# A written table of task order for a linear-attention and MLP kernel, with its streamed tiles at one address phase

## The chip, the cores and the metric

The kernel runs on one core of a Trainium2 chip. The metric is the device time of one execution in microseconds (us). Engines are named as in the profile: PE multiplies matrices (PEld loads its weights), DVE, ACT and POOL work element by element, SP issues most DMAs.

## The reference

```python
def _attn_ref(r, k, v, w, u):             # B, H, S, D = 4, 8, 768, 48
    for t in range(S):
        cur = einsum('bhd,bhe->bhde', u * kt, vt)
        y[:, :, t] = einsum('bhd,bhde->bhe', rt, state + cur)
        state = wt[..., None] * state + einsum('bhd,bhe->bhde', kt, vt)

def _moe_ref(x, w_in, w_out):             # x: 3072 x 384, d_ff = 2048
    h = x @ w_in
    g = where(h > 0, h, exp(min(h, 0)) - 1)
    return g @ w_out

# reference: x = attention output as (B*S, H*D), then _moe_ref
```

## The kernel before

The sequence is cut into 6 chunks of 128 steps. With 4 batch entries that makes 24 **units** (`units`, number i = 4 x chunk + batch). The tokens of one chunk are one MLP **step** of N = 512 columns; the hidden layer is cut into NF = 16 slices f of 128. In chunks 0 and 1 the first six slices are done in two halves of 256 columns (`FH`), so that the MLP can begin when two of the four units are there. That makes 108 pairs of MLP blocks, numbered n = 0 to 107: n = 0 to 21 are chunk 0, 22 to 43 chunk 1, and then 16 for each chunk.

A unit is a set of tasks on several engines. `es` and `gs` (DVE scans, L359 and L369) make decays from the loaded `w`; `rkc` (DVE, L395) makes products for the diagonal in units 0 to 7, `rk` and `rku` (POOL) in the others; `kh` and `rh` (DVE, L376, L373) scale k and r; `pd` (PE, L400), `md` and `sp` (ACT, or POOL) make the diagonal matrix `am`; `s` (PE, L430) makes the scores in `pa_s`; `mk` (DVE, L433, two halves) masks them into `am`; `t` (PE, L438) transposes k and `kt` (ACT, L442) copies it out; `v` (PE, L460) makes the output `pa_y` from `am`, v and the state `st`; `xh` and `xl` (ACT, DVE L470) split it into the two parts that the MLP streams; `u` (PE, L477), `sc` and `up` (DVE) update the state.

An MLP pair is `g1` (PE, L234: nine matmuls into `ph`), `r1` and `r2` (ACT), `stt` (DVE, L245), which together are the ELU, `gh` (ACT, L249) and `gl` (DVE, L253), the split of its result, and `g2` (PE, L264: nine matmuls into `acc`). A product of two fp32 numbers is made of three: high x high, high x low, low x high. The weights are converted once: `raw` loads two tiles of slice f, `a` (ACT, L510), `cc` (DVE, L514, tile `wg`), `wh` (ACT, L518) and `wl` (DVE, L521) make `w_h` and `w_l`, which stay.

What sets the order: every task is entered in `Plan` with its engine, an assumed duration (`COST`), what it follows (`after`) and the buffer slots it takes (`hold`; `SLOTS` says how many there are: 2 of `ph`, `m`, `gh`, `gl`, `w`, 3 of `k`, `r` and of the PSUM tag `pa`, on which `pd`, `s`, `t`, `v`, `u` all draw). `Plan.order` runs a list scheduler over them: each engine takes the ready task with the earliest latest start, worked out from the due times `BEGINS` of the chunks. The kernel is emitted in that order. On the chip an engine runs its own tasks strictly in that order and waits on semaphores; nothing is reordered at run time.

`warm` (L336) is ten matmuls of the identity at the start. For the last chunk `out` copies three tiles of `acc` and issues the stores itself (L269 to L278): tile 0 copied by ACT and issued by SP, tile 1 by DVE and SP, tile 2 in two halves, the first by ACT and ACT's queue, the second by DVE and SP. `guard` and `flags` watch for decays out of range; `general` is a slow path that is not taken here.

Of the kernel before, what the change touches and what calls it, by code (L numbers as in the profile page):

```python
# [54 lines left out]
COST = dict(es=1.5, gs=1.4, pc=0.2, pd=0.6, md=0.22, spa=2.4, rh=0.62, kh=0.62, rk=0.48, rku=0.48, prk=1.1, prku=1.1, dg=0.5, mk=0.7, up=0.7, sc=0.5, xl=0.48,  # L55
            cand=0.5, cv=0.9, wl=0.9, stt=0.6, gl=0.64, fl=1.4, kt=0.5, xh=0.46, a=0.87, wh=0.8, r1=0.58, r2=0.6, gh=0.6,
            sp=1.7, s=1.15, t=0.5, v=1.75, v0=1.1, u=0.5, g=2.12, out=0.6)
LAT = 0.06
DMA_FIRST, DMA_ISSUE, DMA_LAT, DMA_RATE = 1.0, 0.45, 1.9, 215.0
BEGINS = (14.0, 109.9, 197.8, 304.8, 356.4, 464.7, 493.9)  # L60
SOON = 0.0
HALF = 0.0
STAY = 0.0
SWITCH = 0.0
MODES = dict(s=1, v=2, u=3, pd=4)
# [7 lines left out]

class Plan:


    def __init__(self):
        self.tasks, self.holds, self.queue = {}, {}, {}

    def add(self, key, eng, dur, fn, after=(), due=None, start=0.0, lock=False, size=0):  # L80
        self.tasks[key] = dict(key=key, eng=eng, dur=dur, fn=fn, after=list(after), due=due, start=start, lock=lock, size=size)

    def hold(self, pool, taker, users, n=1, fifo=True):
        if taker not in self.tasks:
# [4 lines left out]

    def order(self):  # L90
        ts = self.tasks
        succ = {k: [] for k in ts}
        for k, t in ts.items():
            t["after"] = [d for d in t["after"] if d in ts]
            for d in t["after"]:
                succ[d].append(k)
# [682 lines left out]
```

## Time and profile before

| | us |
|---|---|
| median of 3 runs | 546.36 (544.46 to 551.71) |
| the profiled execution | 549.48 |
| its span, first to last instruction | 547.8 |
| PE busy in it | 521.6 (95%) |
| DVE busy | 338.9 (62%) |
| ACT busy | 287.0 (52%) |
| POOL busy | 66.9 (12%) |

Granted clock of PE over the span: 0.986. DMAs moved 47.34 MB, 86 GB/s on average, but 245 to 297 GB/s in the first 27 us. A busy share is an average over stages with different limits, and matmuls that overlap in the pipeline keep PE "busy" also where it runs at half its rate; so the stages have to be read one by one. In the rows below, "x9" behind a PE row is one MLP block, and a bracket at a row's end is the idle time of the engine before it and what ended it.

### The profile page before, as it was taken

What the parts mean: (1) busy time and instruction counts of PE and PEld (TensorE: products, weight loads), DVE (VectorE), ACT (ScalarE), POOL (GpSimd) and SP (SyncE); (2) the same over time, 40 slices, a digit from 0 to 9 for tenths busy, and PEclk for the clock granted to TensorE, in tenths of its full rate; (3) what the DMA queues carried; (4) which work ended last, traced back from release to release, by engine and by line L of the source; (5) the groups of instructions that cost most, each with busy time, mean ns of one, the idle gap of its engine ahead of it and who ended that gap; (6) DMA issues with size and microseconds to landing.
All of it is one profiled execution on the core that took longest, in us unless ns stands there. A gap on an engine that the chain in (4) does not pass through costs nothing.

```text
span 547.8 us, 9962 instructions
## 1 busy us (share of the span) xinstructions
PE 521.6 (95%) x4065; PEld 431.6 (79%) x4065; DVE 338.9 (62%) x533; ACT 287.0 (52%) x558; POOL 66.9 (12%) x74
## 2 busy tenths in 40 slices
PE   6987999999999998899999999998999999999994
PEld 6776998889888886778888788886778887888883
DVE  5779899966695357994528833357983339333331
ACT  3777899747465434454543634434454453444442
POOL 2000000000620013612005100007300000000000
PEclk9997999999999999899999999999999999999998
DMA  8966661114510026730003400034410012010001
GB/s 245 297 199 212 201 224 67 34 53 151 165 37 2 0 78 184 231 92 17 17 1 109 134 16 1 0 113 150 157 53 1 1 23 70 12 46 1 0 1 62
DMA packets 26739, 47.34 MB, mean 86 GB/s; under 512 B 2752, under 2 KB 9280, under 8 KB 26688
## 3 DMA queue, kind: packets, MB, share of 16 engines
q1 hardware_dynamic: 26544, 46.52, 27.7%
q8 instruction: 34, 0.56, 0.4%
q14 instruction: 17, 0.14, 0.1%
q10 hardware_dynamic: 144, 0.13, 0.1%
HBM read 41.92 MB, written 4.72 MB: 85 GB/s over the span
## 4 chain that ended last, share of the span: by engine, by line
PE 81%; DMA 8%; DVE 6%; issue 2%; ACT 1%; SPq 1%; POOL 0%; DVEq 0%; ACTq 0%
PE ph L234 35%; PE acc L264 34%; PE pa_y L460 6%; DMA k<-in_wkr_dram 5%; PE pa_s L430 3%; DMA wrawx<-in_w_out_dram 1%; DMA wrawx<-in_w_in_dram 1%; PE pa_t L438 1%; PE pa_u L477 1%; DVE eg L359 1%; PE pa_d L400 1%; DVE m L245 1%; DVE k L376 1%; DVE am L433 1%; DMA wraw<-in_w_out_dram 1%
## 5 line engine op out<-in xcount | busy, mean ns | idle before, releaser
L245 DVE SCALAR_TENSOR_TENSOR m<-m,ph 128x512 f32<-128x512 f32 (+1 forms) x108 | 67.1, 624 | 117.5 <-ACT m L242 117.2
L239 ACT ACTIVATE m<-ph 128x512 f32<-128x512 f32 (+1 forms) x108 | 59.3, 549 | 128.8 <-PE ph L234 121.0
L234 PE MATMUL ph<-xh,w_h 128*128 128x512 f32 (+1 forms) x324 | 122.5, 378 | 2.7 <-DVE m L245 2.3
L264 PE MATMUL acc<-gh,w_h 128*128 128x512 f32 (+1 forms) x325 | 122.0, 375 | 0.0
L234 PE MATMUL ph<-xh,w_l 128*128 128x512 f32 (+1 forms) x324 | 120.7, 372 | 1.0 <-DVE w_l L521 1.0
L234 PE MATMUL ph<-xl,w_h 128*128 128x512 f32 (+1 forms) x324 | 120.6, 372 | 0.0
L264 PE MATMUL acc<-gl,w_h 128*128 128x512 f32 (+1 forms) x325 | 120.0, 369 | 0.0
L264 PE MATMUL acc<-gh,w_l 128*128 128x512 f32 (+1 forms) x325 | 119.7, 368 | 0.0
L253 DVE TENSOR_TENSOR gl<-m,gh 128x512 fp32r<-128x512 f32 (+1 forms) x108 | 69.0, 641 | 42.5 <-ACT gh L249 42.4
L249 ACT CAST gh<-m 128x512 fp32r<-128x512 f32 (+1 forms) x108 | 61.3, 569 | 59.1 <-DVE m L245 35.6
L234 PEld LDWEIGHTS ph<-xh,w_h 128*128 128x128 f32 x324 | 62.1, 192 | 15.8 <-DVE m L245 2.8
L234 PEld LDWEIGHTS ph<-xh,w_l 128*128 128x128 f32 x324 | 62.2, 192 | 12.0 <-DVE w_l L521 1.4
L264 PEld LDWEIGHTS acc<-gh,w_h 128*128 128x128 f32 x325 | 61.2, 188 | 12.9 <-issue 1.4
L234 PEld LDWEIGHTS ph<-xl,w_h 128*128 128x128 f32 x324 | 62.2, 192 | 10.8 <-DVE xl L470 0.3
L264 PEld LDWEIGHTS acc<-gh,w_l 128*128 128x128 f32 x325 | 61.1, 188 | 11.3
L264 PEld LDWEIGHTS acc<-gl,w_h 128*128 128x128 f32 x325 | 61.1, 188 | 11.2 <-DVE gl L253 0.6
L242 ACT ACTIVATE m<-m 128x512 f32<-128x512 f32 (+1 forms) x108 | 63.1, 585 | 3.2
L418 POOL TENSOR_SCALAR_AFFINE_SELECT am<-md 128x512 f32<-128x512 f32 x32 | 24.1, 776 | 226.8 <-PE pa_y L460 217.9
L383 POOL TENSOR_TENSOR rk<-rk 128x384 f32<-128x384 f32 x16 | 19.6, 1224 | 164.7 <-DMA rk<-in_rk_dram 164.6
L430 PE MATMUL pa_s<-r,k 48*128 48x128 f32 x384 | 32.2, 304 | 7.7 <-DVE k L376 4.1
L430 PEld LDWEIGHTS pa_s<-r,k 48*128 48x128 f32 x384 | 26.9, 203 | 15.4 <-issue 5.7
L433 DVE COPY_PREDICATED am<-upper,pa_s 128x512 f32<-128x512 uint32 x48 | 32.8, 737 | 7.8 <-PE pa_s L430 7.8
(58 smaller groups left out, 489.6 us busy)
## 6 DMA issues: line engine op xcount, KB each, us to landing
v<-in_vp_dram SPq DMA_DIRECT2D x24, 256.0 KB, 3.1
rk<-in_rk_dram SPq DMA_DIRECT2D x16, 384.0 KB, 4.7
w<-in_wkr_dram SPq DMA_DIRECT2D x24, 226.2 KB, 2.8
k<-in_wkr_dram SPq DMA_DIRECT2D x24, 224.0 KB, 4.3
r<-in_wkr_dram SPq DMA_DIRECT2D x24, 224.0 KB, 3.8
out_dram<-o SPq DMA_DIRECT2D x17, 256.0 KB, 2.3
wrawx<-in_w_out_dram SPq DMA_DIRECT2D x10, 383.8 KB, 4.9
wrawx<-in_w_in_dram SPq DMA_DIRECT2D x10, 383.2 KB, 4.7
```

Of the source, the lines that this page charges most:

```text
L234: nc.tensor.matmul(ph[z:z + COLS], w[:, f, 0, k, z:z + COLS], x_[:, k, :], start=(k == n == 0), stop=(k == NK - 1 and n == 2))
L239: act(s["m"], s["ph"], AF.Relu, scale=-1.0)
L242: act(s["m"], s["m"], AF.Exp, scale=-1.0)
L245: stt_(s["m"], s["m"], -1.0, s["ph"], ALU.add, ALU.max)
L249: nc.scalar.copy(s["gh"], s["m"])
L253: nc.vector.tensor_tensor(s["gl"], s["m"], s["gh"].bitcast(F32), ALU.subtract)
L264: nc.tensor.matmul(a_[z:z + COLS], w[:, f, 1, m, z:z + COLS], g[:, s_], start=(f == n == 0 and lo == 0), stop=(f == NF - 1 and q == parts ...
L383: eng.tensor_tensor(u_["rk"][:, 0], u_["rk"][:, 0], u_["rk"][:, 1], ALU.mult)
L418: nc.gpsimd.affine_select(out=am, in_=u_["md"][:, q::2].unsqueeze(2).broadcast_to([P, NP, C]), pattern=[[0, NP], [1, C]], compare_op=ALU.i ...
L430: nc.tensor.matmul(pa[q][:, p], u_["k"][rs, p, :], u_["r"][rs, p, :], start=True, stop=True)
L433: nc.vector.copy_predicated(u_["am"][q], upper4, u_["pa"][q])
L460: nc.tensor.matmul(py[32 * j:32 * j + 32, k], l, r, start=(n == same[0]), stop=(n == same[-1]))
```

## The change

1. `Plan.order` no longer schedules. A table `ORDER` writes out the tasks of each engine in their order; the new `order` only merges the five lines into one sequence in which every task follows what it depends on and finds its slots free. `COST`, `BEGINS` and all due times are gone. The numbers of blocks, units, slots and instructions of the main path stay as they were.
2. A pool `home` stands right behind the resident weights and a spacer `pad` of 576 bytes. It holds `xh` and `xl` of both kinds of chunk (and the loaded weight tiles that share their room) and `gh` and `gl`. In the built program the byte address within a partition, modulo 2048, was 896 for `xh` and `xl` of chunks 0, 2, 4, 1056 and 1152 for `xh` and `xl` of chunks 1, 3, 5, and 1088 for `gh` and `gl`. It is now 896 for all of them.
3. In the last chunk ACT issues all stores, as three whole tiles: tile 0 behind its own copy; tile 1 behind the copy of tile 2's first half; tile 2 behind DVE's copy of its second half.
4. `warm` writes into an `acc` bank instead of taking a `pa` slot and stands behind `v` of unit 0. `guard`'s arithmetic on DVE is a task `good` of its own. Converted weight tiles take their buffer `wt` in the order of use.

```diff
+ORDER = dict(
+    POOL=(
+        "const rk.9 rk.8 rku.9 rku.8 sp.8 rk.11 rk.10 rku.10 sp.9 sp.10 rku.11 rk.12 sp.11 rk.13 rku.13 rku.12 rk.15 "
...
     def order(self):
-        ts = self.tasks
-        succ = {k: [] for k in ts}
...
-        return [ts[k] for k in order]
+        ts, rings, turns, done, order = self.tasks, {}, {}, set(), []
...
+        while any(lines.values()):
+            n = len(order)
+            for e, line in lines.items():
+                while line and fits(line[0]):
+                    k = line.pop(0)
...
+                    done.add(k)
+                    order.append(ts[k])
+        return order
...
+    def g_tile(n, s):
+        return gp.tile([P, N], F32R, tag=n, name=n, bufs=2)[:, 0:s["hi"] - s["lo"]]
...
-        s["gh"] = ml.tile([P, N], F32R, tag="gh", name="gh", bufs=2)[:, 0:s["hi"] - s["lo"]]
+        s["gh"] = g_tile("gh", s)
...
-        parts = 2 if m == NK - 1 and last else 1
-        for q in range(parts):
-            s_ = slice(q * N // parts, (q + 1) * N // parts)
-            (nc.vector.tensor_copy if last and (m == 1 or q) else nc.scalar.copy)(o[:, m, s_], acc[m][:, s_])
-            if last:
-                (nc.scalar if m == NK - 1 and q == 0 else nc.sync).dma_start(dst[m * P:(m + 1) * P, s_], o[:, m, s_])
+        if not last:
+            nc.scalar.copy(o[:, m], acc[m])
+        elif m == 0:
+            nc.scalar.copy(o[:, m], acc[m])
+            send(m)
+        elif m == 1:
+            nc.vector.tensor_copy(o[:, m], acc[m])
+        else:
+            h = N // 2
+            nc.scalar.copy(o[:, m, 0:h], acc[m][:, 0:h])
+            send(1)
+            nc.vector.tensor_copy(o[:, m, h:N], acc[m][:, h:N])
+            send(m)
+
+    def send(m):
+        nc.scalar.dma_start(dst[m * P:(m + 1) * P], box["o"][:, m])
...
+    pad, home = pool("pad", 1), pool("home", 1)
...
+    pad.tile([P, PAD // 4], F32, name="pad")
...
     def warm():
-        pw = ps_a.tile([P, P], F32, tag="pa", name="pw")
         for _ in range(WARM):
-            nc.tensor.matmul(pw, ident, ident, start=True, stop=True)
+            nc.tensor.matmul(first["accs"]()[0][:, 0:P], ident, ident, start=True, stop=True)
...
-            xts[c] = [at.tile([P, NK, N], F32R, tag=n + str(c % 2), name=n, bufs=1) for n in ("xh", "xl")]
+            xts[c] = [home.tile([P, NK, N], F32R, tag=n + str(c % 2), name=n, bufs=1) for n in ("xh", "xl")]
```

What the table moves is seen best in three places. The first is PE at the start of the program, before:

```order
L339 MATMUL pw<-ident 128x128 x10
L400 MATMUL pa_d<-ubd,rkc 128x2 x8
L438 MATMUL pa_t<-ident,k 128x112 x4
L430 MATMUL pa_s<-r,k 128x128 x16
L460 MATMUL pa_y<-am,v 32x128 x16
L400 MATMUL pa_d<-ubd,rkc 128x2 x4
L460 MATMUL pa_y<-am,v 32x128 x16
L477 MATMUL pa_u<-v,kt 48x48 x8
L438 MATMUL pa_t<-ident,k 128x112 x4
L400 MATMUL pa_d<-ubd,rkc 128x2 x4
L234 MATMUL ph<-xh,w_h 128x256
```

And PE at the same place now:

```order
L428 MATMUL pa_d<-ubd,rkc 128x2 x8
L466 MATMUL pa_t<-ident,k 128x112 x4
L458 MATMUL pa_s<-r,k 128x128 x8
L428 MATMUL pa_d<-ubd,rkc 128x2 x4
L458 MATMUL pa_s<-r,k 128x128 x8
L488 MATMUL pa_y<-am,v 32x128 x16
L367 MATMUL acc_276<-ident 128x128 x10
L488 MATMUL pa_y<-am,v 32x128 x16
L505 MATMUL pa_u<-v,kt 48x48 x8
L466 MATMUL pa_t<-ident,k 128x112 x4
L248 MATMUL ph<-xh,w_h 128x256
```

The ten matmuls of `warm` (`pw`, now `acc`) went from the front to a place between the outputs of units 0 and 1, and the diagonal `pa_d` of unit 3 went behind the first MLP blocks.

The second place is DVE in front of the `xl` of unit 3 (the second `xl` here, the last in its fence), which the second half of chunk 0's MLP needs. Before:

```order
L433 COPY_PREDICATED am<-upper,pa_s 128x512 x2
L245 SCALAR_TENSOR_TENSOR m<-m,ph 128x256
L470 TENSOR_TENSOR xl<-pa_y,xh 128x3x128
L514 SCALAR_TENSOR_TENSOR wg<-wraw,wt_96 128x768
L253 TENSOR_TENSOR gl<-m,gh 128x256
L245 SCALAR_TENSOR_TENSOR m<-m,ph 128x256
L514 SCALAR_TENSOR_TENSOR wg<-wrawx,wt_97 128x768
L253 TENSOR_TENSOR gl<-m,gh 128x256
L470 TENSOR_TENSOR xl<-pa_y,xh 128x3x128
```

And DVE there now:

```order
L270 TENSOR_TENSOR gl<-m,gh 128x256
L423 TENSOR_TENSOR rkc<-r,k 112x512
L498 TENSOR_TENSOR xl<-pa_y,xh 128x3x128
L259 SCALAR_TENSOR_TENSOR m<-m,ph 128x256
L552 SCALAR_TENSOR_TENSOR w_l<-wg,w_h 128x768
L270 TENSOR_TENSOR gl<-m,gh 128x256
L259 SCALAR_TENSOR_TENSOR m<-m,ph 128x256
L498 TENSOR_TENSOR xl<-pa_y,xh 128x3x128
```

Two weight conversions (`wg`, slices 6 and 7) that stood ahead of this `xl` now stand behind it, and an `rkc` of unit 4 stands ahead of it.

The third place is DVE where chunk 1's MLP goes over into chunk 2's, before:

```order
L253 TENSOR_TENSOR gl<-m,gh 128x512
L359 SCALAR_TENSOR_TENSOR eg<-w,reset 112x516
L368 RECIPROCAL reset<-eg 112x4
L369 SCALAR_TENSOR_TENSOR eg<-w,reset 112x516
L376 TENSOR_TENSOR k<-k,eg 112x512
L485 TENSOR_TENSOR st<-st,pa_u 48x4x48 x2
L359 SCALAR_TENSOR_TENSOR eg<-w,reset 112x516
L433 COPY_PREDICATED am<-upper,pa_s 128x512 x2
L485 TENSOR_TENSOR st<-st,pa_u 48x4x48 x2
L390 TENSOR_REDUCE md<-rk 128x8
L373 TENSOR_TENSOR r<-r,eg 112x512
L376 TENSOR_TENSOR k<-k,eg 112x512
```

And DVE from the two scans of units 12 and 13, which stand there now:

```order
L387 SCALAR_TENSOR_TENSOR eg<-w,reset 112x516 x2
L396 RECIPROCAL reset<-eg 112x4
L397 SCALAR_TENSOR_TENSOR eg<-w,reset 112x516
L498 TENSOR_TENSOR xl<-pa_y,xh 128x3x128
L259 SCALAR_TENSOR_TENSOR m<-m,ph 128x512 x2
L270 TENSOR_TENSOR gl<-m,gh 128x512
L259 SCALAR_TENSOR_TENSOR m<-m,ph 128x512
L396 RECIPROCAL reset<-eg 112x4
L397 SCALAR_TENSOR_TENSOR eg<-w,reset 112x516
L513 TENSOR_TENSOR st<-st,pa_u 48x4x48 x2
L270 TENSOR_TENSOR gl<-m,gh 128x512
L418 TENSOR_REDUCE md<-rk 128x8
```

Before, the unit's work stands in one row of some twenty instructions without an MLP instruction between them; now it alternates with `m` and `gl` of the MLP. The same holds on PE: `s` of units 9, 10 and 11 stood behind `g1` of pairs 42, 42 and 43, and now stand behind those of pairs 38, 40 and 41; the number of times that PE goes from MLP blocks to attention and back is 42 before and now.

More of the change, by code (lines that the diff above doesn't have):

```diff
@@ L52 @@
 PIECES = _pieces()
[L55 to L65, printed above, removed]
+COLS = 128
+PAD = 576
 FILL = {}
-COLS = 128
-LEAD = 111.0
 DIAG = ["PE"] * 8 + ["POOL"] * 16
@@ L71 @@
 SLOTS = dict(w=2, k=3, r=3, rk=2, v=4, eg=2, md=2, am=2, kt=1, pa=3, wg=2, wt=2, ph=2, m=2, gh=2, gl=2, x=2, acc=1, raw0=1, x0=1, x1=1, x1a=1, x1b=1)
+ORDER = dict(
+    POOL=(
[3 rows of a table added]
+    SP=(
[13 rows of a table added]
+    ACT=(
[26 rows of a table added]
+    DVE=(
[27 rows of a table added]
+    PE=(
[16 rows of a table added]
+)
 class Plan:
     def __init__(self):
-        self.tasks, self.holds, self.queue = {}, {}, {}
-    def add(self, key, eng, dur, fn, after=(), due=None, start=0.0, lock=False, size=0):
-        self.tasks[key] = dict(key=key, eng=eng, dur=dur, fn=fn, after=list(after), due=due, start=start, lock=lock, size=size)
@@ L212, with mlp @@
 ROUNDS = value_rounds()
-def mlp(nc, w_h, w_l, ps_acc, ps_h, ml, po, dst, last=False):
+def mlp(nc, w_h, w_l, ps_acc, ps_h, ml, gp, po, dst, last=False):
     act, stt_ = nc.scalar.activation, nc.vector.scalar_tensor_tensor
@@ L596, in rwkv_elu_kernel @@
-    n0, prev = 0, None
+            add(("raw", f, z), "SP", lambda f=f, z=z: load_w(f, z), [("raw", f, 0)] if z else [])
+        add(("a", f), "ACT", lambda f=f: conv_a(f), [("raw", f, 0), ("raw", f, 1), ("const",)])
+        add(("cc", f), "DVE", lambda f=f: conv_c(f), [("a", f), ("const",)])
+        add(("wh", f), "ACT", lambda f=f: conv_h(f), [("cc", f)])
+        add(("wl", f), "DVE", lambda f=f: conv_l(f), [("wh", f)])
     seq = []
     for c in range(NC):
-        fns = mlp(nc, w_h, w_l, ps_acc, ps_h, ml, stg, out[:, c * N:(c + 1) * N], last=c == NC - 1)
-        t = BEGINS[c]
-        pace = (BEGINS[c + 1] - t) / NF
+        fns = mlp(nc, w_h, w_l, ps_acc, ps_h, ml, home, stg, out[:, c * N:(c + 1) * N], last=c == NC - 1)
@@ L649, in rwkv_elu_kernel @@
         hold("raw0", ("out", c, 0), [("store", c, m) for m in range(NK)])
-    add(("guard",), "PE", 0.3, guard, [("fl", i) for i in range(NU)], due=BEGINS[-2] + 15)
-    hold("pa", ("guard",), [("guard",)], fifo=False)
+    add(("guard",), "PE", guard, [("fl", i) for i in range(NU)])
+    add(("good",), "DVE", is_good, [("guard",)])
+    hold("pa", ("guard",), [("good",)])
     with tc.manual_schedule():
         for t in plan.order():
+            k = t["key"]
+            if k in FILL and (k[0] != "g1" and k[1] < 2 or k == ("g1", 0)):
+                for _ in range(FILL[k]):
+                    nc.tensor.matmul(first["accs"]()[0][:, 0:P], ident, ident, start=True, stop=True)
             t["fn"]()
```

273 lines of the change are left out of this document (98 added, 175 removed), and 84 rows, old and new, of tables (ACT, DVE, PE, POOL).

## The prediction

> **What bounds the kernel now.** I read the engines' busy time first, then the stages in windows, then the chain of work that ended last. The engines' line says PE is the bound:
>
> ```profile
> PE 521.6 (95%) x4065; PEld 431.6 (79%) x4065; DVE 338.9 (62%) x533; ACT 287.0 (52%) x558; POOL 66.9 (12%) x74
> ```
>
> That is an average. I cut the span at four starts of MLP blocks: the first `g1` (30.26), the first `g1` of chunk 0's second halves (59.11), the first `g1` of chunk 1 (119.87), the last matmul's end (540.7). The columns are stretch and length, then busy time of PE, PEld, DVE, ACT, POOL with instructions, granted clock, share of the DMA engines, GB/s:
>
> ```profile
> 0.00:30.26 30.26, 23.01 (x172) 20.26 (x173) 21.47 (x34) 18.41 (x43) 3.67 (x10) 1.00 0.93 272
> 30.26:59.11 28.85, 24.94 (x226) 22.28 (x226) 23.62 (x40) 21.57 (x46) 0.00 (x0) 0.88 0.64 204
> 59.11:119.87 60.76, 60.76 (x462) 52.30 (x461) 55.01 (x84) 48.60 (x99) 0.00 (x0) 1.00 0.36 113
> 119.87:540.70 420.83, 412.87 (x3211) 336.72 (x3209) 238.34 (x376) 198.02 (x371) 63.26 (x64) 1.00 0.20 61
> 540.70:547.80 7.10, 0.00 (x0) 0.00 (x0) 0.45 (x2) 0.37 (x1) 0.00 (x0) 0.67 0.34 118
> ```
>
> So there are three regimes. Up to 59 us no engine is full: the kernel waits along chains (loads, DVE, ACT, PE in turn), and PE works part of it at half rate. From 59 to 120 PE has no idle time. From 120 on PE is the bound, with 420.83 - 412.87 = 8.0 us of idle time, which the chain shows where chunks change. At the end stand 7.1 us of copies and stores.
>
> **Part 1, the addresses.** In the chain a row "x9" is one block, and in the middle of a chunk nothing stands between two blocks. Chunk 4 comes first here, then chunk 5:
>
> ```profile
> 408.65 2.06 PE ph L234 x9
> 410.72 2.10 PE acc L264 x9
> ...
> 511.38 2.09 PE ph L234 x9
> 513.47 2.09 PE acc L264 x9
> ```
>
> The same instructions take 2.06 us with `xh` and `xl` at 896 (chunk 4) and 2.09 with 1056 and 1152 (chunk 5); `gh` and `gl` at 1088 take 2.09 to 2.10 in both. If 896 is what makes 2.06, each of the 84 full `g2` gains 0.04 us and each of the 42 full `g1` of chunks 1, 3 and 5 gains 0.03: 3.4 + 1.3 = **4.7 us**, all of it on the bound engine. For the half blocks, whose rows I can't tell apart, I take nothing. Bounds: 0, and 6 us if the halves gain too and the best blocks fall below 2.06.
>
> A rule of the Trainium skill speaks against this term: SBUF — State Buffer, section "Who interferes with whom", says that PE has read ports of its own and never waits on anyone, and it knows no cost of an operand's place. By it the term would be 0. The rows 2.06 and 2.09 differ with the place alone as far as I can see, so the trace disagrees; I keep that case among the rivals.
>
> **Part 2, the start.** Two costs of waiting show here. One is the wait, the other is the half rate behind it:
>
> ```profile
> 28.56 1.84 PE L400 MATMUL pa_d<-ubd,rkc 112*128 112x2 f32 x8 [1.41 <-DVE rkc L395]
> ...
> 44.05 1.16 PE L430 MATMUL pa_s<-r,k 48*128 48x128 f32 x16 [0.19 <-issue]
> ...
> 47.86 2.73 PE L430 MATMUL pa_s<-r,k 48*128 48x128 f32 x16 [2.11 <-ACT kt L442]
> 50.52 1.93 PE L460 MATMUL pa_y<-am,v 128*32 128x128 f32 x32
> ```
> ```profile
> 30.40 4.06 PE ph L234 x18
> ...
> 59.27 2.15 PE ph L234 x18
> ```
>
> `s` takes 1.16 us before the wait of 2.11 and 2.73 behind it; two half blocks of `g1` take 4.06 us at 30.40 and 2.15 at 59.27.
>
> A second rule is TensorE: Matmul & The Clock Gate, "What's actually happening": the array's clock doubles after some 3.4 us of steady work, and falls back after an idle window of as long. By it the 2.11 us would have cost only themselves. The row behind them is at half rate, so here I go by the row.
>
> What moves. (a) The first loads: `w` of unit 1 is the first issue, where a weight tile was; the first scan waited for its load behind it:
>
> ```profile
> 0.82 0.44 SPq L506 DMA_DIRECT2D wraw<-in_w_in_dram  x1
> 1.31 0.47 SPq L353 DMA_DIRECT2D w<-in_wkr_dram  x1
> ...
> 5.57 1.23 DVE L359 TENSOR_TENSOR_SCAN eg<-w,reset 112x516 f32<-112x516 f32 x1 [3.27 <-DMA w<-in_wkr_dram]
> ```
>
> The page gives a median of 2.8 us from issue to landing for such a load, so I put the first scan at 3.6. (b) Ahead of the `xl` of unit 1, on which the first `g1` waits, stand four more tasks of units 2 and 3 and a `wl`, some 5.3 us, while `up` of unit 0 and `rkc` of unit 3 (1.4) went behind it:
>
> ```profile
> L359 DVE TENSOR_TENSOR_SCAN eg<-w,reset 112x516 f32<-112x516 f32 x24 | 32.3, 1346 | 4.5 <-DMA w<-in_wkr_dram 4.2
> L369 DVE TENSOR_TENSOR_SCAN eg<-w,reset 112x516 f32<-112x516 f32 x24 | 30.7, 1278 | 0.8
> L373 DVE TENSOR_TENSOR r<-r,eg 112x512 f32<-112x512 f32 x24 | 19.0, 791 | 2.1 <-DMA r<-in_wkr_dram 2.0
> L376 DVE TENSOR_TENSOR k<-k,eg 112x512 f32<-112x512 f32 x24 | 18.1, 753 | 9.3 <-DMA k<-in_wkr_dram 9.2
> L521 DVE SCALAR_TENSOR_TENSOR w_l<-wg,w_h 128x768 fp32r<-128x768 f32 x16 | 14.9, 951 | 0.5 <-ACT w_h L518 0.3
> ```
>
> DVE had done some 20 us by that `xl`, 1.3 of them memsets before any load; now about 24. From 3.6 without a pause that gives 26.3; with 1.5 to 2 of waits the first `g1` starts near **28 instead of 30.26: 2 us**. (c) `warm` stood where it warmed nothing that lasted:
>
> ```profile
> 1.43 4.64 PE L339 MATMUL pw<-ident 128*128 128x128 f32 x20 [1.43 <-POOL ident masks.py:199]
> ```
>
> Now it runs, some 4 us, between the outputs of units 0 and 1, while DVE is still at the mask of unit 1; I expect the first two `g1` at full rate, **2 us** (4.06 to 2.15). If that cover is gone, it delays the first `g1` by up to 4.6. (d) Behind them the new DVE line has two `wg` fewer ahead of the `xl` of unit 3, and `t` of unit 2, whose copy `kt` PE then waited for, stands behind `s` and `v` of unit 3. The wait and its half rate cost 2.11 + (2.73 - 1.16) + 0.9 for `v` + 1.0 for the half block behind, 5.6 us. I count **4 of the 5.6**, since the new line must have some waits of its own. Sum: 8 us; the second halves start near **51 instead of 59.11**. DVE doesn't forbid it: it had been busy 21.47 + 23.62 = 45.1 us by 59.11, has about 2.5 less to do there, and could be ready at 46. Bounds: 0, and 13 for that earliest start.
>
> A wait is added on SP: `w` of unit 2 is its eighth issue and needs the slot of unit 1's `w`, free after `gs` at about 6.3; behind it stands the first weight tile, issued at 0.82 before. Its conversion `cc` stands behind the first mask on DVE, at 16 or later, and that hides it; if not, the first `g1` comes as much later.
>
> From 59 to 120 PE does 60.76 us of work in 60.76; the new line has about as much, so the 8 us are carried on. DVE is at 55 of 60.76 there and stays just below PE.
>
> **Part 3, the changes of chunks.** Loads of k end most of the idle time:
>
> ```profile
> 143.28 5.01 DMA k<-in_wkr_dram
> 211.97 3.35 DMA k<-in_wkr_dram
> ...
> 377.60 5.02 DMA k<-in_wkr_dram
> 389.78 4.12 DMA k<-in_wkr_dram
> ```
> ```profile
> 207.59 1.67 PE pa_y L460 x56
> 219.79 2.97 PE pa_y L460 x56
> ```
>
> 8.0 us of idle time, and 1.3 at half rate (2.97 for 1.67): 9.3. In the new table the units' work alternates with MLP blocks and k is loaded earlier among the issues, and `g2` runs two or three blocks behind `g1`, where it ran one. The chain from `g1` to `g2` is `r1`, `r2`, `stt`, `gh`, `gl`, some 3.2 us, so a block of 2.1 more to hide it is a cushion. A fixed order with some 100 hand-overs will still wait somewhere: I keep a third, so **6 us** gained. Bounds: 9.3 gained, and a loss that is the third rival.
>
> PE goes between attention and MLP 42 times before and now, so that cost stays. The old scheduler also held DVE and POOL apart (`lock`); the table has no such rule. What that costs is in one row:
>
> ```profile
> L253 DVE TENSOR_TENSOR gl<-m,gh x108: 392/692/1271, 37.3 to 537.2; 128x512 fp32r<-128x512 f32 x84, 128x256 fp32r<-128x256 f32 x24
> ```
>
> A `gl` of 1271 ns instead of 692 is 0.6 late and is hidden by the lag of two blocks; I take 0, up to 2 us if it falls on a lag of one.
>
> **Part 4, the stores.** The last store was a half tile from SP:
>
> ```profile
> out_dram<-o SPq DMA_DIRECT2D x17, 256.0 KB, 2.3
> ...
> out_dram<-o ACTq DMA_DIRECT2D x1, 128.0 KB, 2.3
> out_dram<-o SPq DMA_DIRECT2D x1, 128.0 KB, 3.6
> ```
>
> Three whole tiles from ACT: 3.6 becomes about 2.3 to 3, and ACT's issue of tile 1 (0.38) runs beside DVE's last copy. ACT then waits for that copy; nothing is queued behind but the read of the flag. **0.7 us**, between a loss of 1 and a gain of 1.3.
>
> `good`, `wt` in the order of use and the split of `guard` lie beside PE's blocks: nothing.
>
> **The sum.** 4.7 + 8 + 6 + 0.7 = 19.4. The profiled execution took 549.48 us (span 547.80 and 1.68 around it), 3.1 above the median 546.36, so a profile of the new kernel would show about 530, and its median **527**.
>
> **Rivals.**
> *The stages' gain is lost to DVE.* For: DVE is busy 55.01 of 60.76 from 59 to 120, and must do the same conversions and units in a stretch that starts 8 us earlier; then the first `g1` of chunk 1 comes as late as before, and part 2 gives nothing, the changes of chunks perhaps half: 527 + 8 + 3 = 538. Against: all DVE work up to that point is 100 us, and it could be done at 104.
> *The place of a tile costs nothing* (the SBUF page's rule): the 0.03 comes from something else that alternates with chunks. Then part 1 is 0: 532. Against: the weights, the code and the shapes are the same.
> *More waits, and slower.* In the fixed lines `s` or `v` of a unit stands between two MLP blocks, while its `kh` or mask stands on DVE behind an `stt` that waits for ACT. A wait of 2.1 with the half rate behind it costs 5.6 (part 2). If every one of the five changes of chunks gets such a wait at two units more than before, that is 10 x 5.6 = 56 against 19 gained: 583; it is slower than before from the fourth such wait on, and by 2% from the sixth. Against: the lag of two to three blocks.
> *More gain.* No waits at the changes (3.3 more) and second halves at 47 (4 more): 520.
> That the table doesn't reorder is excluded by the rows above.
>
> **How the numbers follow.** Forecast, 527 give or take 6: 0.5. Lost to DVE, 533 to 543: 0.2. Place costs nothing, 532: 0.11. More gain, 515 to 521: 0.12. Slower: 0.07. The range 516 to 543 leaves out the slower case and the ends of the bounds (13 for the start, 1 for the stores). About 2% is what a measurement of this kernel can tell from no change; 2% faster is under 535.4. The forecast, the gain and the place case lie there, and a quarter of the DVE case: 0.76, and I say 0.72, since the waits of a fixed order are the term I see least.
>
> **What would show it.** Blocks of 2.06 for `acc` and for `ph` in all chunks; the first `ph` at 28 and the second halves at 51; PE idle after 120 under 4 us; the last store landing 2.3 to 3 us after its issue. I am wrong if PE's idle rows in the middle name `kh`, masks or `m` on DVE with 2 us each, or if the blocks of `acc` stay at 2.10.

## The result, and the profile after

The changed kernel took **520.49 us** (median of 4 runs, 518.4 to 521.86) beside 546.93 for the kernel before (4 runs): a ratio of 0.950, 95% interval 0.943 to 0.958. Its profiled execution took 521.82 us, span 520.1. In what follows the kernel before was run again beside each group of kernels; its median lay between 546.9 and 550.6, so a difference of 1 or 2 us between medians of different groups says little, and for such sizes I read the stages of the profiles instead. Medians are of fast runs alone, which leaves out one run (548.6 us) of the kernel with the old order.

The engines' line, and the same stages as in the prediction, cut at the first `g1` (25.20), the first `g1` of the second halves (47.22), the first `g1` of chunk 1 (108.51) and close to the last matmul's end (513.55; it ends at 513.60):

```profile
PE 502.2 (97%) x4065; PEld 423.7 (81%) x4065; DVE 331.2 (64%) x533; ACT 276.1 (53%) x558; POOL 66.0 (13%) x74
```
```profile
0.00:25.20 25.20, 17.06 (x165) 15.42 (x165) 21.47 (x33) 17.21 (x41) 3.67 (x10) 1.00 0.92 272
25.20:47.22 22.02, 20.23 (x226) 18.79 (x225) 20.36 (x36) 18.12 (x42) 0.00 (x0) 0.92 0.81 254
47.22:108.51 61.29, 61.29 (x491) 53.85 (x489) 55.06 (x87) 49.47 (x101) 0.00 (x0) 1.00 0.44 136
108.51:513.55 405.04, 403.60 (x3193) 335.68 (x3192) 233.86 (x379) 190.95 (x376) 62.37 (x64) 1.00 0.21 64
513.55:520.10 6.55, 0.05 (x1) 0.00 (x0) 0.49 (x2) 0.37 (x1) 0.00 (x0) 0.88 0.35 125
```

The second halves start 11.9 us earlier (47.22, before 59.11), and what stands between them and chunk 1 takes as long as before (61.29 and 60.76), so 11.4 of it are left at chunk 1. From there to the end of PE it takes 405.0 us, before 420.8: 15.8 less. PE's idle time there is 405.04 - 403.60 = 1.4 us, before 8.0, and its busy time is 9.3 less. At the end 0.6 is won. The loads of `k` that stood in the chain before are gone from it; one load is left there, of `r`:

```profile
402.36 4.63 DMA r<-in_wkr_dram
```

The next rows are the chain in the middle of chunk 4, then of chunk 5:

```profile
415.28 2.04 PE ph L248 x9
417.32 2.04 PE acc L281 x9
...
486.82 2.04 PE ph L248 x9
488.87 2.04 PE acc L281 x9
```

In the middle of both chunks `g1` and `g2` are alike now, and shorter than the shortest before (2.06 to 2.10). The start of the MLP in PE's rows:

```profile
20.36 2.50 PE L367 MATMUL acc<-ident 128*128 128x128 f32 x20
22.79 1.08 PE L488 MATMUL pa_y<-am,v 128*32 128x128 f32 x32
23.80 0.56 PE L505 MATMUL pa_u<-v,kt 128*48 128x48 f32 x16
24.82 0.60 PE L466 MATMUL pa_t<-ident,k 112*128 112x112 f32 x4 [0.46 <-DVE xl L498]
25.20 0.36 PE L248 MATMUL ph<-xh,w_h 128*128 128x256 f32 x1
26.76 0.40 PE L248 MATMUL ph<-xl,w_h 128*128 128x256 f32 x1 [1.20 <-DVE xl L498]
```
```profile
26.70:28.00 1.30, 1.24 (x6) 1.24 (x7) 1.29 (x4) 0.07 (x1) 0.00 (x0) 0.61 1.09 388
28.00:29.00 1.00, 1.00 (x7) 1.00 (x6) 0.90 (x2) 0.31 (x1) 0.00 (x0) 0.50 0.88 341
```

The first `g1` begins at 25.20; its second matmul, which needs the `xl` of unit 1, comes at 26.76. The granted clock, full at `v` of unit 1 (1.08 us), falls to 0.50 in the first two blocks: they run at half rate all the same.

### The profile page after: what moved, and what is told of

Read it like the earlier page. It is cut to its first block, busy times and chain, and to the rows that moved or that the text cites. A ratio compares the mean times of both kernels' runs of the same rounds, so it can differ in the third digit from the quotient of the medians.

```text
span 520.1 us, 10015 instructions
## 1 busy us (share of the span) xinstructions
PE 502.2 (97%) x4065; PEld 423.7 (81%) x4065; DVE 331.2 (64%) x533; ACT 276.1 (53%) x558; POOL 66.0 (13%) x74
## 4 chain that ended last, share of the span: by engine, by line
PE 86%; DVE 5%; ACT 2%; issue 1%; DMA 1%; SPq 0%; DVEq 0%; ACTq 0%
PE ph L248 36%; PE acc L281 36%; PE pa_y L488 6%; PE pa_s L458 4%; PE pa_u L505 2%; PE pa_t L466 1%; DVE m L259 1%; DMA r<-in_wkr_dram 1%; PE pa_d L428 1%; DVE gl L270 1%; DVE am L461 1%; ACT gh L266 0%; DVE r L401 0%; ACT m L256 0%; DVE xl L498 0%
## 5 line engine op out<-in xcount | busy, mean ns | idle before, releaser
L281 PE MATMUL acc<-gh,w_h 128*128 128x512 f32 (+1 forms) x325 | 120.7, 371 | 0.0
L248 PE MATMUL ph<-xl,w_h 128*128 128x512 f32 (+1 forms) x324 | 119.4, 369 | 1.2 <-DVE xl L498 1.2
L248 PE MATMUL ph<-xh,w_l 128*128 128x512 f32 (+1 forms) x324 | 119.5, 369 | 0.0
L248 PEld LDWEIGHTS ph<-xl,w_h 128*128 128x128 f32 x324 | 61.8, 191 | 10.5 <-DVE xl L498 1.4
L411 POOL TENSOR_TENSOR rk<-rk 128x384 f32<-128x384 f32 x16 | 17.8, 1115 | 221.9 <-DMA rk<-in_rk_dram 221.9
L461 DVE COPY_PREDICATED am<-upper,pa_s 128x512 f32<-128x512 uint32 x48 | 34.5, 744 | 16.9 <-PE pa_s L458 16.7
L446 POOL TENSOR_SCALAR_AFFINE_SELECT am<-md 128x512 f32<-128x512 f32 x32 | 27.7, 889 | 134.8 <-PE pa_y L488 101.0
L387 DVE TENSOR_TENSOR_SCAN eg<-w,reset 112x516 f32<-112x516 f32 x24 | 29.3, 1226 | 3.8 <-DMA w<-in_wkr_dram 3.2
L408 ACT ACTIVATE junk<-eg,lim 112x1032 bf16<-112x1032 f32 x24 | 27.7, 1155 | 7.3 <-DVE eg L397 7.2
```

Source lines behind the costliest of these rows:

```text
L248: nc.tensor.matmul(ph[z:z + COLS], w[:, f, 0, k, z:z + COLS], x_[:, k, :], start=(k == n == 0), stop=(k == NK - 1 and n == 2))
L281: nc.tensor.matmul(a_[z:z + COLS], w[:, f, 1, m, z:z + COLS], g[:, s_], start=(f == n == 0 and lo == 0), stop=(f == NF - 1 and q == parts ...
L387: nc.vector.tensor_tensor_scan(out=flat(eg[:, 0]), data0=u_["w"][:, 1:W1][:, ::-1], data1=flat(reset[:, 0]), initial=0.0, op0=ALU.mult, op ...
L408: act(junk, u_["eg"].rearrange("d z p t -> d (z p t)"), AF.Relu, bias=lim, accum_out=flags[:, u_["i"]:u_["i"] + 1])
L446: nc.gpsimd.affine_select(out=am, in_=u_["md"][:, q::2].unsqueeze(2).broadcast_to([P, NP, C]), pattern=[[0, NP], [1, C]], compare_op=ALU.i ...
L461: nc.vector.copy_predicated(u_["am"][q], upper4, u_["pa"][q])
```

## The experiments

My theory was that four things pay apart from each other: the addresses, the order up to 47 us, the order at the changes of chunks, and the last stores. Rivals: the shorter blocks are a gift of the calmer order; the later order works only with the early one ahead.

**The whole order of before, the rest new.** `ORDER` holds the old sequence of each engine:

```diff
-        "pd.0 pd.1 t.0 s.0 pd.2 s.1 v.0 warm v.1 u.0 t.1 g1.0 g1.1 pd.3 g1.2 s.2 u.1 g2.0 g1.3 g2.1 s.3 v.2 v.3 t.2 g1.4 "
+        "warm pd.0 pd.1 t.0 s.0 s.1 v.0 pd.2 v.1 u.0 t.1 pd.3 g1.0 g1.1 u.1 g1.2 g1.3 g2.0 g2.1 g1.4 g2.2 s.2 t.2 s.3 v.2 "
...
```

> The changed kernel with one thing put back: the table holds the order of the kernel before on all five engines; the addresses, the warm tile and the last stores stay new. Theory (address, early order, order at the chunk changes and last stores pay apart): second halves start near 59 us, g1.22 near 119 us, the 512-column matmuls at 227 ns instead of 233, time 547 - 5 (addresses) - 0.5 (tail) = 541 to 542. Rival A (the shorter blocks come from the calmer order, the place costs nothing): blocks stay at 2.09 to 2.10 us, time 546 to 547. Rival B (the place is worth more than it looks in the old order): below 538.

**The old order up to `g1.22` only.** Each engine's line begins as in the kernel before and goes over into the new one; PE's, where it does:

```diff
-        "g2.18 g1.21 g2.19 pd.6 g1.22 g2.20 g1.23 g2.21 g1.24 g1.25 pd.7 s.6 u.4 g2.22 g1.26 g2.23 t.5 g1.27 g2.24 s.7 "
+        "v.5 g2.20 u.3 t.4 pd.6 g1.22 g1.23 g2.21 g1.24 g1.25 pd.7 s.6 u.4 g2.22 g1.26 g2.23 t.5 g1.27 g2.24 s.7 v.6 u.5 v.7 "
```

> The changed kernel with the order of the kernel before on every engine up to the first g1 of chunk 1 (g1.22), and the new order behind it; new addresses and stores. Theory: g1.22 starts near 119 us instead of 108.5, and from there to the end of TensorE 405 to 406 us as in the changed kernel: 119.5 + 405.5 + 6.6 = 531 to 532. Rival C (the new order of the later chunks only works because its early part is ahead): the stretch behind g1.22 takes 410 us or more, time 536 or more. Rival D (a late start is made good later, since something else sets the end): 525 or less.

**The new order with the old places.**

```diff
-    pad, home = pool("pad", 1), pool("home", 1)
...
-            xts[c] = [home.tile([P, NK, N], F32R, tag=n + str(c % 2), name=n, bufs=1) for n in ("xh", "xl")]
+            xts[c] = [at.tile([P, NK, N], F32R, tag=n + str(c % 2), name=n, bufs=1) for n in ("xh", "xl")]
...
-        fns = mlp(nc, w_h, w_l, ps_acc, ps_h, ml, home, stg, out[:, c * N:(c + 1) * N], last=c == NC - 1)
+        fns = mlp(nc, w_h, w_l, ps_acc, ps_h, ml, ml, stg, out[:, c * N:(c + 1) * N], last=c == NC - 1)
```

> The changed kernel with the tiles back in their old pools: xh, xl of the even chunks at 896 modulo 2048, of the odd chunks at 1056, gh and gl at 1088; order and stores new. Theory: 512-column matmuls of g2 at 233 ns, of g1 in odd chunks at 232, 256-column ones of g2 at 115 to 117 instead of 120; full blocks of g2 at 2.10 us; time 520.5 + 5 = 525 to 526. Rival A (the order made the blocks shorter): blocks stay at 2.05, time 520 to 521.

| kernel | us | ratio to before | second halves | `g1.22` | end of PE |
|---|---|---|---|---|---|
| before | 547.6 | | 59.1 | 119.9 | 540.7 |
| old order, new places and stores | 542.65 | 0.990 (0.986 to 0.993) | 57.9 | 118.3 | 533.0 |
| old order up to `g1.22` | 532.17 | 0.972 (0.965 to 0.979) | 56.4 | 119.5 | 522.5 |
| new order, old places | 525.66 | 0.959 (0.952 to 0.966) | 45.8 | 107.2 | 517.5 |
| changed kernel | 520.49 | 0.950 (0.943 to 0.958) | 47.2 | 108.5 | 513.6 |

Going down the table without the fourth row, the places and the stores bring 5.0 us (3.6 to 7.4 by the interval of the ratio), the later order 10.5, the early order 11.7. These three add up to the whole by the way they are read. What can be checked is whether the places are worth the same in both orders: from `g1.22` to the end of PE they take 6.1 us off in the old order (420.8 to 414.7) and 5.2 in the new one (410.3 to 405.1), and taking them back out of the changed kernel costs 5.2 in the medians too. The theory's times are met within 1 us; two of its stages are not (second halves at 57.9 for 59 with the old order, and 403.1 us behind `g1.22` for 405 to 406 with the old order up to there). Rivals A to D fall. In the windows behind `g1.22`, first the kernel with the old order throughout, then the one with the old order only up to there:

```profile
118.30:533.02 414.72, 407.62 (x3211) 337.49 (x3209) 238.80 (x376) 197.84 (x371) 61.82 (x64) 1.00 0.21 62
```
```profile
119.47:522.54 403.07, 401.65 (x3184) 333.99 (x3183) 231.10 (x374) 188.21 (x370) 63.42 (x64) 1.00 0.20 63
```

Idle time is 7.1 us in the one and 1.4 in the other. The busy time differs by 6.0 more; part of it is slowed work behind waits, as in the chain of the first of the two, where the same 56 matmuls of `v` take

```profile
206.02 1.67 PE pa_y L485 x56
217.95 2.56 PE pa_y L485 x56
```

and some is work that now stands ahead of `g1.22` (3184 matmuls for 3211). The old places in the new order (chunk 5) read nearly as before:

```profile
483.81 2.09 PE acc L281 x9
485.90 2.11 PE ph L248 x9
```

They are not quite the old ones: by the expectation above, `xh` and `xl` of the odd chunks lay at 1056 here, where `xl` lay at 1152 before. The odd `g1` take 2.114 us on average (30 blocks), 2.090 before, so up to 42 x 0.024 = 1.0 us of the 5.2 may be a place that the kernel before did not have.

**Which places are good.** Two kernels with three pools instead of one (`homes`: x of the odd chunks, x of the even ones, `gh` and `gl`), a pad ahead of each, and with the old form of the last stores:

```diff
-    pad, home = pool("pad", 1), pool("home", 1)
+    pads, homes = zip(*((pool(f"pad{n}", 1), pool(f"home{n}", 1)) for n in range(3)))
...
-    pad.tile([P, PAD // 4], F32, name="pad")
+    for p_, z_ in zip(pads, PADS):
+        p_.tile([P, z_ // 4], F32, name="pad")
```

> The changed kernel with other places: modulo 2048, xh and xl of the odd chunks at 128, of the even chunks at 512, gh and gl at 1152; and with the last stores as before. Read per 512-column matmul. Theory E (a start on a multiple of 128 bytes is what counts; 896 is one, 1056 and 1088 are none): all three places take 227 ns, 256-column ones 120. Theory F (896 alone, or a narrow stretch round it): all three 232 to 234, 256-column ones 115 to 118. Theory G (moving and streamed tiles must share one place): all three slow. Stores: from the end of TensorE to the end of the span 7.1 us as before, against 5.1 to 6.6 with the new ones.

> As the run before with the odd chunks' x at 384, the even ones' at 960, gh and gl at 1408. Theory E: 384 and 1408 take 227 ns per 512 columns, 960 (64 behind a multiple of 128) 232 to 234. Theory F: 960, 64 bytes from 896, may be fast, 384 and 1408 are slow. Theory G: all slow. Stores: 7.1 us from the end of TensorE to the end.

And one in which the streamed tiles stay at 896 and the weights move, by 128 bytes ahead of `w_h`:

```diff
+    keep("pad0", 1).tile([P, 32], F32, name="pad0")
     big = keep("big", 1)
-PAD = 576
+PAD = 448
```

> The changed kernel with the resident weights 128 bytes further on (256 modulo 2048 instead of 128) and the streamed tiles where they are, at 896. In the runs so far every place that was 128 modulo 256 gave 227 ns per 512-column matmul, and the weights lay there too. Theory H (the tile's own place counts): blocks as in the changed kernel, 2.05 to 2.06 us. Theory I (what counts is how the tile lies to the weights): 2.09 to 2.10 us in all full blocks, half blocks 1.05 to 1.06, time some 5 us longer.

One profile each (523.09, 524.18 and 526.5 us). Mean length of full blocks that have no attention work next to them, from start to start, worked out from 24 to 35 blocks for each figure:

| kernel | `g1` even chunks | `g1` odd chunks | `g2` in even, odd chunks |
|---|---|---|---|
| before | 896: 2.057 | 1056, 1152: 2.090 | 1088: 2.104, 2.097 |
| changed | 896: 2.049 | 896: 2.058 | 896: 2.056, 2.047 |
| first scan | 512: 2.098 | 128: 2.058 | 1152: 2.070, 2.048 |
| second scan | 960: 2.077 | 384: 2.059 | 1408: 2.089, 2.047 |
| weights 128 bytes on | 896: 2.097 | 896: 2.105 | 896: 2.097, 2.094 |

In the chain of the first scan (even chunk, then odd) and of the kernel with the moved weights:

```profile
426.66 2.06 PE acc L281 x9
428.72 2.09 PE ph L248 x9
...
485.09 2.04 PE acc L281 x9
487.13 2.04 PE ph L248 x9
```
```profile
482.50 2.10 PE ph L248 x9
484.59 2.09 PE acc L281 x9
```

896 is nothing special: 128, 384, 1152 and 1408 are as good, 512 and 960 are not, so theories E (512 is a multiple of 128), F and G fall. The good five are all 128 modulo 256. And a good place becomes a bad one when only the weights move, so the tile's own place does not decide alone, and theory H falls. Theory I is met in the full blocks (2.094 to 2.105), but not in the half blocks: they take 1.070 to 1.076 us, where 1.05 to 1.06 was expected. A row of 128 weights is 512 bytes and began at 128 modulo 512 in all kernels but the last. So two readings are left: that the distance from tile to weights counts, or that each of the two has to lie at 128 modulo 256. A tile at 0 modulo 256 beside the moved weights would tell them apart; it was not tried.

One more thing stands in the profiles: a block is also slower when the blocks next to it lie badly. `g2` at a good place takes 2.089 where the `g1` between are at a bad one. The even chunks' `g1` lay at 896 in all the kernels of the first table; with the old places it takes 2.057 in the old order and 2.064 in the new, with the new places 2.042 and 2.049. So it is the places around it that changed it, and not the order.

**The start: the first loads.** The first half of weight tile 0 is issued first again:

```diff
-        "ld_w.1 ld_k.0 ld_r.0 ubd ld_w.0 ld_k.1 ld_r.1 ld_w.2 raw.0.0 ld_r.2 ld_k.2 raw.0.1 raw.2.0 raw.2.1 ld_v.0 "
+        "raw.0.0 ld_w.1 ld_k.0 ld_r.0 ubd ld_w.0 ld_k.1 ld_r.1 ld_w.2 ld_r.2 ld_k.2 raw.0.1 raw.2.0 raw.2.1 ld_v.0 "
```

> The changed kernel with one load put back to its old place: the first weight tile's half (raw.0.0, 393 KB) is issued ahead of the rows of the first units. Theory (VectorE is dense up to xl.3, so its first scan sets the start): first scan at 5.6 us instead of 3.9, xl.3 at 48 instead of 46.4, second halves at 48.9 instead of 47.2, time 522. Rival (the conversions of weight 0, earlier then, fill the gap, or slack behind hides it): second halves within 0.5 us of 47.2, time 520 to 521.

520.43 us; second halves at 46.7. By these two numbers the rival holds. DVE's rows of the changed kernel, then of this one:

```profile
3.88 1.23 DVE L387 TENSOR_TENSOR_SCAN eg<-w,reset 112x516 f32<-112x516 f32 x1 [1.57 <-DMA w<-in_wkr_dram]
...
13.50 0.69 DVE L423 TENSOR_TENSOR rkc<-r,k 112x512 f32<-112x512 f32 x1 [0.85 <-DMA k<-in_wkr_dram]
```
```profile
5.54 1.23 DVE L387 TENSOR_TENSOR_SCAN eg<-w,reset 112x516 f32<-112x516 f32 x1 [3.24 <-DMA w<-in_wkr_dram]
...
14.23 0.69 DVE L423 TENSOR_TENSOR rkc<-r,k 112x512 f32<-112x512 f32 x1
```

Of the 1.7 us that the first scan is late, more than half is back by the third `rkc`, since the load that DVE waited for there is no longer late for it. At the end of the `xl` of unit 1 0.7 is left (27.4 for 26.7). That the rest is gone by 47 has another reason: here the first two `g1` ran at full rate, and in the profile of the changed kernel at half rate, behind which DVE waits twice for ACT's part of these blocks. DVE's rows of the changed kernel, then of this one:

```profile
29.55 0.42 DVE L259 SCALAR_TENSOR_TENSOR m<-m,ph 128x256 f32<-128x256 f32 x1 [0.61 <-ACT m L256]
...
31.89 0.42 DVE L259 SCALAR_TENSOR_TENSOR m<-m,ph 128x256 f32<-128x256 f32 x1 [0.45 <-ACT m L256]
```
```profile
29.70 0.42 DVE L259 SCALAR_TENSOR_TENSOR m<-m,ph 128x256 f32<-128x256 f32 x1
...
31.51 0.41 DVE L259 SCALAR_TENSOR_TENSOR m<-m,ph 128x256 f32<-128x256 f32 x1
```

The other profiles bear this out. From the second matmul of the first `g1` to the second halves it takes 20.5 us in the changed kernel (26.76 to 47.22) and 20.4 in the second scan, which ran at half rate too. It takes 19.2 to 19.3 in this kernel, the one with the old places, the first scan and both runs of the better version below, and 19.5 in the one with the moved weights; all of these ran at full rate, with the same order on PE and DVE. So the half rate costs 1.2 us at the second halves. The kernels that ran at full rate with the first loads in the new order start them at 45.3 to 45.9, this one at 46.7: read at full rate the earlier loads are worth some 1 us, by one profile of each kernel. The changed kernel's own times are in line with this: 518.4 and 519.2 us at a mean granted clock of 1.000 and 0.998, 521.8 and 521.9 at 0.995.

**The start: `warm` and the half rate.**

```diff
-        "pd.0 pd.1 t.0 s.0 pd.2 s.1 v.0 warm v.1 u.0 t.1 g1.0 g1.1 pd.3 g1.2 s.2 u.1 g2.0 g1.3 g2.1 s.3 v.2 v.3 t.2 g1.4 "
+        "warm pd.0 pd.1 t.0 s.0 pd.2 s.1 v.0 v.1 u.0 t.1 g1.0 g1.1 pd.3 g1.2 s.2 u.1 g2.0 g1.3 g2.1 s.3 v.2 v.3 t.2 g1.4 "
```

> The changed kernel with the warming matmuls back at the front of TensorE's line. Theory (VectorE sets the start of the second halves, a slow TensorE in between is hidden): g1.0 and g1.1 at half rate, about 4.1 us for both, second halves within 1 us of 47.2, time 520 to 522. Rival (term (c) of the prediction: what the place of the warming saves, TensorE pays at once): second halves 2 to 4 us later, time 523 to 525.

```diff
-FILL = {}
+FILL = {("t", 1): 4, ("g1", 0): 12}
```

> The changed kernel with 4 matmuls of the identity put ahead of t.1 and 12 ahead of g1.0, in the stretch where TensorE waited 0.5 and 1.2 us for xl.0 and xl.1. Theory (the pause is what halves the clock): no half-rate matmuls between 26 and 31 us, g1.0 and g1.1 1.1 us each after xl.1; second halves at 45.8 to 46.7, time 519.5 to 520.5. Rival (the fillers stand in the way of work that could start): first g1 1 us or more later, second halves not before 47.2, time 520.5 to 522.

`warm` at the front: 520.05 us, second halves at 45.9. With fillers: 521.01, second halves at 47.6. PE's rows with `warm` at the front, then with the fillers:

```profile
24.98 1.01 PE L466 MATMUL pa_t<-ident,k 112*128 112x112 f32 x4
26.62 0.39 PE L248 MATMUL ph<-xl,w_h 128*128 128x256 f32 x1 [0.38 <-DVE xl L498]
```
```profile
25.76 2.86 PE L687 MATMUL acc<-ident 128*128 128x128 f32 x24
```

Neither place nor filler is worth anything that these runs show. With `warm` in front PE is slow until 26 (`t` takes 1.01 us, not 0.60), but DVE's `xl` comes no later (its end is at 26.6, in the changed kernel at 26.7). Against the theory the first two `g1` run at full rate (17 matmuls from 26.62 to 28.9), since the granted clock, 0.50 from 10 to 25.5, is at 1.00 from 26.6; why it rose just then the runs don't show. The second halves start where they do with `warm` in its new place and the blocks at full rate (45.3 to 45.9). The fillers kept the clock at 1.00, as the theory said, and pushed the first `g1` to 28.4, as the rival said; two half-rate blocks and two late ones cost about the same at the second halves (47.2 and 47.6).

**DVE's work at the start, moved to POOL.** Five products are taken out of DVE's line and put behind `const` in POOL's:

```diff
+MOVED = [('rh', 2), ('rkc', 3), ('kh', 3), ('rh', 3), ('rkc', 4)]
...
-        "const rk.9 rk.8 rku.9 rku.8 sp.8 rk.11 rk.10 rku.10 sp.9 sp.10 rku.11 rk.12 sp.11 rk.13 rku.13 rku.12 rk.15 "
+        "const rh.2 rkc.3 kh.3 rh.3 rkc.4 rk.9 rk.8 rku.9 rku.8 sp.8 rk.11 rk.10 rku.10 sp.9 sp.10 rku.11 rk.12 sp.11 rk.13 rku.13 rku.12 rk.15 "
...
+    on = lambda k, fn, u_: ("POOL", lambda: fn(u_, nc.gpsimd.tensor_tensor)) if k in MOVED else ("DVE", lambda: fn(u_, tt))
```

> The changed kernel with five of VectorE's 112x512 products of the start moved to GpSimd (rh.2, rkc.3, kh.3, rh.3, rkc.4), which does nothing from 4 to 108 us. Theory (VectorE's 42 of 46 us set the second halves): 5 x 0.6 us off VectorE; second halves 2 to 3 us earlier, near 44.5, time 517.5 to 518.5. Rival (the two engines get in each other's way: r<-r,eg took 987 ns under a GpSimd operation instead of 685, st<-st,pc 1179 instead of 552): 7.5 us of GpSimd work slow VectorE by 2 us or more, second halves 46 to 47.5, time 519.5 to 521.

521.22 us (ratio 0.952, 0.949 to 0.955), second halves at 47.3: the rival, and more. The first two `g1` ran at full rate here (granted clock 1.00), so the kernels to compare with are those that start the second halves at 45.3 to 45.9: the move cost some 1.5 us there. DVE's rows of this kernel and POOL's:

```profile
19.93 1.94 DVE L553 SCALAR_TENSOR_TENSOR w_l<-wg,w_h 128x768 fp32r<-128x768 f32 x1
...
25.46 0.96 DVE L553 SCALAR_TENSOR_TENSOR w_l<-wg,w_h 128x768 fp32r<-128x768 f32 x1
...
32.89 1.95 DVE L553 SCALAR_TENSOR_TENSOR w_l<-wg,w_h 128x768 fp32r<-128x768 f32 x1
```
```profile
19.25 1.80 POOL L402 TENSOR_TENSOR r<-r,eg 112x512 f32<-112x512 f32 x1 [13.91 <-DMA w<-in_wkr_dram]
25.52 2.05 POOL L424 TENSOR_TENSOR rkc<-r,k 112x512 f32<-112x512 f32 x1 [4.48 <-DMA r<-in_wkr_dram]
...
32.74 1.29 POOL L402 TENSOR_TENSOR r<-r,eg 112x512 f32<-112x512 f32 x1 [3.31 <-DVE eg L398]
```

A `wl` that begins while POOL multiplies takes 1.94 instead of 0.95; the one that began just ahead of POOL's takes 0.96, and POOL's 2.05 instead of 1.29. One waits for the other. Four `wl` lost 1.0, 0.6, 1.0 and 0.9 us, 3.5 in all, which is more than the five products had freed (5 x 0.6).

**A better version.** In the old places the half blocks were the shorter ones: `g2` 1.05 us, now 1.08. `gh` and `gl` of half blocks can begin 48 columns into their tiles, at 1088:

```diff
+SHIFT = 48
...
+        o, m = (SHIFT if s["hi"] - s["lo"] < N else 0), s["hi"] - s["lo"]
-        return gp.tile([P, N], F32R, tag=n, name=n, bufs=2)[:, 0:s["hi"] - s["lo"]]
+        return gp.tile([P, N], F32R, tag=n, name=n, bufs=2)[:, o:o + m]
```

> The changed kernel where gh and gl of the half blocks begin 48 columns into their tiles, at 1088 modulo 2048, and those of the full blocks stay at 896. Theory (256-column matmuls are shorter where 512-column ones are longer, in any order): g2 of the half blocks 1.045 to 1.056 us instead of 1.078, 0.6 us over 24 blocks; full blocks unchanged. Rival (the shorter half blocks of the old places came from the x tiles or the order): 1.075 to 1.08.

> The kernel with gh and gl of the half blocks at 1088 once more, timed against the kernel before, as the best version that the runs point to. Theory: 0.6 to 1 us less than the changed kernel's 520.5, so 519 to 520, and a ratio of 0.947 to 0.950; its single run of 517.5 was a good start (second halves at 45.3), not the new tiles. Rival: the shorter half blocks also bring the start forward, 517 to 518.

Once 517.53 us, then timed **518.53** (6 runs, 517.59 to 519.83), ratio 0.946 (0.943 to 0.950). In the profile of the single run half blocks of `g2` take 1.050 and 1.062 us (chunk 0 and chunk 1, means of 5 to 7 blocks; 1.078 and 1.077 in the changed kernel), `g1` between them 1.060 to 1.065 instead of 1.078 to 1.080; the rival (1.075 to 1.08) falls. In the chain of chunk 0, first changed, then shifted (the timed one):

```profile
57.09 1.08 PE ph L248 x9
58.17 1.08 PE acc L281 x9
```
```profile
57.51 1.07 PE ph L249 x9
58.58 1.04 PE acc L283 x9
```

That is 24 x 0.022 + 24 x 0.016 = 0.9 us by these means. The median is 2 us below the changed kernel's, between what the theory (519 to 520) and the rival (517 to 518) had for it, but the two were not timed side by side and their intervals overlap. The blocks are shown; the rest of the 2 us can't be put down to the new tiles. Between the two profiles (521.82 and 518.33 us) 1.5 us lie ahead of the second halves, where only the changed kernel's ran at half rate, 1.3 behind the end of PE, where its last store took longer to land (4.0 us and 2.6), and 0.7 between, where the half blocks are.

## Why the prediction came out as it did

527 was forecast, 516 to 543 the range; 520.5 is what the rival "more gain" named.

*Part 1, the addresses: 4.7 forecast, 5.2 measured* by putting the old places back, up to 1.0 of which may be `xl` of the odd chunks at a place that it did not have before. The size is right for partly wrong reasons, and so in part by luck: 2.06 was not the floor (2.04 to 2.06), the even `g1` gained a little too, and the half blocks, at which I counted nothing, lost 0.02 to 0.03 each in `g2`. That 896 by itself makes a block short is wrong: with the weights moved it does not. The rule of the Trainium skill, "SBUF — State Buffer", section "Who interferes with whom" there, gives no price to a place; by it this part is 0, and the 5.2 us and the rows of 2.04 for 2.10 decide against it.

*Part 2, the start: 8 forecast, 11.4 to 11.9 measured.* One profile is good to 1 or 2 us here: with the old order up to `g1.22` the second halves start at 56.4 to 59.1 (3 profiles), with the new one at 45.3 to 47.6 (11). The mechanism (DVE's line ahead of the `xl` of units 1 and 3) is right. The `xl` of unit 3 ends at 46.4, before at 58.1, and the 11.7 us between, added up from DVE's rows, are: 1.7 of an earlier first scan (3.88, before 5.57), 3.1 of less busy time from there on (39.86, before 42.94) and 6.9 of less waiting (2.64, before 9.58). The step that failed is "I count 4 of the 5.6, since the new line must have some waits of its own", and with it the 1.5 to 2 of waits in (b): the line kept 2.6 us of waits up to 46, and the start came within 1.2 us of the 46 that I had put as the earliest. The first `g1`, which I had at 28, began at 25.2 and went on behind its wait at 26.8. Of the pieces, (a) is worth some 1 us by itself, which the half rate hid in the comparison with the changed kernel's profile (first loads swapped back: 520.43). (c) is wrong: the first two `g1` ran at half rate again in that profile and `warm`'s place is worth nothing (520.05). The half rate does have a price, 1.2 us at the second halves for the 2 that I had put on it, and the changed kernel paid it. So the 2 us of (c) were paid by (b) and (d); which of the moves in them took DVE's waits away was not taken apart.

*Part 3, the changes of chunks: 6 forecast, 10.5 measured*, above even the 9.3 that I had as the bound. "I keep a third" failed: the idle time fell from 8.0 to 1.4. And the sum of waits had one slowed block (1.3 us) in it, where more blocks around waits are slowed, and left out that some units' work moved ahead of `g1.22`; how the last 4 us divide between these I can't tell.

*Part 4, the stores: 0.7 forecast, 0.6 in this profile, but not where I put it.* The last store took longer than before, not less:

```profile
out_dram<-o ACTq DMA_DIRECT2D x1, 256.0 KB, 4.0
```

In 11 profiles with the new stores the last landing took 2.6 to 4.0 us, in the 3 with the old ones 2.6 to 3.6. What differs is the time from that landing to the end of the span: 1.6 in all 11, against 2.6, 3.5 and 4.0. From PE's end to the span's it is 5.7 us on average against 7.4, so the change is worth some 1.7 us, more than forecast. Why SP's own stores end the program later was not tried.

*The rivals.* DVE did not give the start back (55.06 busy of 61.29, PE without a pause). More waits did not come: PE's single waits behind 108 us are 1.0 us and less. The price of 5.6 for a wait with the half rate behind it was too high a rule: in this profile waits of 0.46 and 1.20 were followed by 3.8 us at half rate, of which 1.2 us reached the second halves.

*The sums.* Three are slightly off, and none changes the forecast: the gains of part 1 are 3.36 + 1.26 = 4.6, the five tasks in (b) come to 5.1 by the means shown, and the chances named for 2% faster add up to 0.78, where 0.76 stands.

## What to carry to other kernels

When a stage is bound by one engine's line of work, what counts is the work that stands ahead of the one result that others need: 3.1 us less of it, 6.9 us less waiting and 1.7 us of an earlier first task on DVE moved the whole program by some 11.5, while warming and fillers beside it moved nothing. Before two profiles are compared for 1 us, look whether both ran the stage at the same clock: 1.2 us of half rate in one of them hid what the first loads (some 1 us) and the products on POOL (some 1.5) had done. Do not discount a fixed order for waits that you can't name: look in the order for what would wait. And before a block's length is taken as given, try the places of its operands; one profile with several places tells more than a timing.

## What the runs showed that I had not expected

- A 512-column matmul of the MLP (operands in fp32r) takes 227 ns from start to start (median) with the tile at 128 modulo 256 and the weights' rows at 128 modulo 512, and mostly 230 to 235 otherwise (226 to 232 at 960). For 256 columns it is 120 ns there and 114 to 118 at 1088, but 118 to 120 at 512 and beside the moved weights, so the reverse holds at some places only.
- The same wait is not always followed by half rate: after 1.20 us for the same `xl` the matmuls of the kernel with the old places ran on at full rate, those of the changed kernel, with 0.46 more shortly before, did not, and those of the second scan, with 0.35 and 1.20, did not either. The Trainium skill, "TensorE: Matmul & The Clock Gate", section "What's actually happening", says that the gate counts in windows of some 3.4 us that run freely; that the same wait ends both ways agrees, that 1.7 us of waits suffice does not agree with an idle window of that length.
- DVE's `wl`, with both inputs in SBUF, and POOL's products exclude each other (0.95 to 1.94), while the `xl` that ran beside one of them, with an input in PSUM, took 0.57, as in the changed kernel without POOL's products. The Trainium skill, "SBUF — State Buffer", section "Who interferes with whom", says that a DVE instruction with two SBUF inputs contends with a GpSimd instruction that reads SBUF, that the lock on the ports they share is exclusive, and that the order of issue decides which of the two is blocked; the rows agree.
